# Polysketch attention followed by a rational MoE layer: own PSUM buffers for parts of the first key sketches, two first loads exchanged, w_out loaded in 4 KB pieces, and a new instruction order

## The chip, the cores and the metric

The kernel runs on one core of a Trainium2 chip. The core has five engines with a queue each: TensorE (PE; its weight loads are listed apart as PEld), VectorE (DVE), ScalarE (ACT), GpSimd (POOL) and SyncE (SP), which here issues most of the DMAs. Each engine works through its own instructions in order and waits on semaphores for the others. The metric is the device time of one execution in microseconds; the kernel before took 274.04 us (median of three, 273.96 to 274.2).

## The reference

Attention with polynomial sketches over 4 batches of 4 heads, 1088 tokens and 32 features each, then one feed-forward layer on all 4352 tokens with 128 features and 2048 hidden units:

```python
def phi(x):
    a = np.einsum('rd,bhsd->bhsr', S1, x)      # r = 8
    b = np.einsum('rd,bhsd->bhsr', S2, x)
    return np.einsum('bhsi,bhsj->bhsij', a, b).reshape(*x.shape[:-1], r * r)
q_p, k_p = (phi(q), phi(k))
kv = np.einsum('bhsf,bhsd->bhfd', k_p, v)
z = np.sum(k_p, axis=2)
x = (q_p @ kv) / (q_p . z + 1e-06)              # per token and head
h = x @ w_in
P = a[0] + a[1]*h + a[2]*h**2 + a[3]*h**3
Q = 1.0 + abs(b[0])*abs(h) + abs(b[1])*h**2
out = (P / (Q + 1e-06)) @ w_out
```

(Put together from the two functions of the reference; between them the heads' outputs are laid side by side, 128 features per token.)

## The kernel before

Everything is one list of steps, `ORDER` (lines 21 to 57), written out by an earlier search: each entry `name:i` calls one small function, and the instructions go to the engines' queues in just that order. Nothing is reordered afterwards, so `ORDER` fixes the order on each engine.

**Keys** (class `Keys`): of a batch `b`, `kt0..kt3` are 32x32 transposes on DVE (L251), `ks` the sketches on PE (L257), `kc` the copy of one sketch factor to SBUF on ACT (L264), `kf` the outer product `k_p` on DVE (L269), `kp` the products with `v` on PE (L298), `kk` the copy of `kv` on ACT (L308, L310). The first batch is cut into three parts, so that work can start on the first rows: part 0 holds two tiles of 128 tokens, part 1 two, part 2 five. `k_p` has two buffers.

**Queries** (classes `Queries`, `Spread`): `qt` transpose on DVE (L321), `qs` sketches on PE (L334, L402), `qc` copy on ACT (L341, L344, L408), `qf` product on DVE (L350, L353, L425), `qp` products with `kv` on PE (L361), `qd`, `qi`, `qx` denominator, reciprocal and quotient on DVE or ACT (L369 to L381), `qb` transpose back on PE (L387), `qk` copy to `xT` on ACT (L391). The blocks 0 to 3 belong to the first batch. In a `Spread` block the copies travel to DRAM and back to be spread over the partitions (L413 to L419, by SP).

**The layer**: 17 units (`units`), each a tile of 128 partitions x 4096 columns (hidden blocks times tokens). Unit 0 and the two last have 256 tokens, the others 512. `h0..h3` are the hidden matmuls into a PSUM tile of 1024 columns (L448), `e` their copy to bf16 on ACT (L454), `u`, `w`, `y` (L477, L483, L488) build Q on DVE, `ln` and `ex` (L539, L543) give `r = 1/Q` on ACT, `pa` or `pd` (L534, L529) a linear term on ACT or DVE, `s`, `m`, `v`, `x` (L547 to L562) the products on DVE, `G` (L581) the matmuls with the three scaled copies of `w_out`, `st` the store (L590, L598). `wo:0` to `wo:5` (L610 to L618) make the three bf16 copies of `w_out` in halves; `W_ENG` says which of them run on ACT (1) or DVE (0).

**PSUM**: the pool `att` has four tiles of 512 columns (`bank`), the pool `hps` two of 1024 columns (`wide`). The first batch's key sketches and the first two query sketches all take `wide` tiles.

**Loads**: the first batch's keys come in three DMAs: rows for the first four tiles (L144, on SP), the rest of three quarters (L146, on ACT's queue), the rest of the last quarter (L148, on ACT's queue). `lq`, `lk`, `lv`, `lw` (w_out in two halves), `lx` (w_in in two halves) are DMAs on SP at their place in `ORDER`. `w_out` is read with row `fo*128 + fi` on partition `fi`, that is in rows of 512 bytes.

`tn:i` puts `TURNS[i]` matmuls on zeros into PE's queue.

Of the kernel before, what the change touches and what calls it, by code (L numbers as in the profile page):

```python
# [16 lines left out]
PSUM = bass.MemoryType.PSUM  # L17


TURNS = (10, 2, 0, 0, 2, 0, 0, 0, 0)  # L20
ORDER = """
tn:4 tn:0 lw:1 kt0:0 lq:0 kt2:0 lw:0 kt3:0 lx:1 kt1:0 ks0:0 lk:1 qt:0 ks2:0 kc0:0 lx:0 kf0:0 ba:0 qt:1 tn:1 kc2:0 qs:0
kf2:0 kp0:0 qc:0 ks1:0 qf:0 kc1:0 kf1:0 qs:1 wo:1 qt:3 kp1:0 qc:1 kp2:0 qf:1 qt:2 qs:3 wo:4 kk:0 lq:1 lv:1 wo:2 qp:0
wo:0 qs:2 qd:0 wo:5 qi:0 qx:0 qc:2 qb:0 qf:2 qk:0 wo:3 qp:1 kt0:1 qc:3 h2:0 qd:1 qi:1 qx:1 qt:5 h3:0 e2:0 qt:4 kt1:1
qp:2 e3:0 h1:0 pa1:0 u1:0 w1:0 h0:0 y1:0 qd:2 e1:0 qi:2 qx:2 qs:4 e0:0 qb:1 qb:2 qt:6 ks1:1 qk:1 u0:0 qk:2 ln1:0 w0:0
ks0:1 y0:0 h1:1 lk:2 kc1:1 ex1:0 lq:2 kf1:1 h3:1 e1:1 s1:0 kc0:1 h0:1 e3:1 kf0:1 pa0:0 m1:0 h2:1 qf:3 e0:1 x1:0 qp:3
qc:4 e2:1 kt0:2 h0:2 ln0:0 u1:1 kt1:2 h1:2 w1:1 e0:2 ex0:0 y1:1 ks0:2 h2:2 e1:2 s0:0 qd:3 ln0:1 h3:2 qi:3 m0:0 e2:2
lk:3 qx:3 kp1:1 x0:0 e3:2 ex0:1 u1:2 qb:3 lv:2 G0:0 pd0:1 qk:3 w1:2 ln1:1 G1:0 G2:0 qf:4 G3:0 kc0:2 kk:1 y1:2 ex1:1
G4:0 G5:0 kf0:2 qp:4 ln0:2 s0:1 qs:5 G0:1 qd:4 qc:5 qi:4 ex0:2 qt:7 G1:1 qx:4 m0:1 qb:4 ks1:2 qk:4 s1:1 pa1:1 h2:3
s0:2 kc1:2 m1:1 h3:3 e2:3 kf1:2 h1:3 e3:3 st:0 x1:1 ln1:2 qs:7 x0:1 h0:3 e1:3 kt1:3 m0:2 h2:4 e0:3 pd1:2 pa0:2 u1:3  # L30
h3:4 qt:9 w1:3 e2:4 G2:1 ex1:2 x0:2 h0:4 qf:5 e3:4 kp1:2 s1:2 pa0:3 y1:3 h1:4 qc:7 e0:4 m1:2 ln0:3 qp:5 kt0:3 e1:4
G3:1 x1:2 ex0:3 G4:1 m0:3 G5:1 u1:4 ks0:3 qd:5 ln1:3 qi:5 G0:2 w1:4 G1:2 pa1:3 qx:5 G2:2 y1:4 lv:3 qb:5 G3:2 qk:5
ex1:3 h0:5 m1:3 v0:3 kk:2 ln0:4 h2:5 s1:3 e0:5 qs:6 G4:2 qf:7 ex0:4 h1:5 x0:3 qt:8 qc:6 e2:5 s0:4 e1:5 h3:5 pd0:4
pa1:4 m0:4 h1:6 v1:3 e3:5 x0:4 G5:2 ln1:4 u1:5 h3:6 st:2 e1:6 w1:5 qp:7 ex1:4 x1:3 h0:6 e3:6 y1:5 qd:7 pa0:5 lq:3 G0:3
G2:3 qi:7 s1:4 h2:6 e0:6 m0:5 ln0:5 m1:4 qs:8 G3:3 e2:6 qf:6 G5:3 x1:4 ex0:5 G0:4 u1:6 G1:4 qc:8 ln1:5 qp:6 v0:5 qx:7
w1:6 qb:7 qd:6 G2:4 pa0:6 qi:6 G3:4 qx:6 y1:6 qb:6 qk:7 G4:4 qk:6 ex1:5 h3:7 m0:6 pa1:5 G5:4 qt:10 s1:5 h1:7 e3:7 st:4
h2:7 e1:7 m1:5 ln0:6 x0:5 h0:7 e2:7 x1:5 qs:9 e0:7 h3:8 qf:8 ex0:6 u1:7 h1:8 v0:6 qc:9 ln1:6 w1:7 ks1:3 s0:6 e1:8 G0:5
y1:7 kc1:3 qp:8 ex1:6 h2:8 pd1:6 kc0:3 e3:8 s1:6 ln0:7 h0:8 kf0:3 e2:8 m1:6 G2:5 ex0:7 G3:5 x0:6 G4:5 kf1:3 qd:8 e0:8
qs:10 G5:5 ln1:7 qi:8 u1:8 kp1:3 qx:8 pa0:7 w1:8 qb:8 G0:6 qf:9 qk:8 y1:8 qc:10 h3:9 ex1:7 s0:7 h2:9 e3:9 s1:7 ln0:8
h0:9 m0:7 e2:9 x1:6 G2:6 e0:9 h1:10 x0:7 ex0:8 pd1:7 h1:9 m1:7 pa0:8 s0:8 G3:6 e1:9 u1:9 G0:7 qt:11 ln1:8 qp:9 qt:12  # L40
u0:9 m0:8 h3:10 e1:10 w1:9 qd:9 ex1:8 qf:10 h2:10 x0:8 e3:10 G4:6 x1:7 e2:10 h0:10 y1:9 kk:3 pa0:9 w0:9 qp:10 qi:9
y0:9 e0:10 G1:7 qx:9 qd:10 ln0:9 s1:8 qb:9 G5:6 qi:10 u1:10 G2:7 qk:9 ex0:9 G3:7 qx:10 m1:8 qb:10 G4:7 qk:10 ln1:9
pd1:8 h1:11 s0:9 w1:10 ex1:9 qs:11 h0:11 m0:9 e1:11 x1:8 G5:7 qc:11 e0:11 h3:11 y1:10 pa1:9 h2:11 s1:9 e3:11 ln0:10
x0:9 G0:8 h0:12 m1:9 e2:11 pd0:10 ex0:10 h1:12 u1:11 x1:9 G1:8 ln1:10 w1:11 G0:9 G2:8 e1:12 s0:10 G3:8 e0:12 y1:11
h2:12 ex1:10 G4:8 m0:10 ln0:11 G1:9 qf:11 G5:8 s1:10 ex0:11 h3:12 x0:10 pa1:10 m1:10 qs:12 G2:9 s0:11 G3:9 e2:12 G4:9
pd0:11 qc:12 ln1:11 m0:11 qp:11 x1:10 G5:9 e3:12 x0:11 G0:10 qd:11 ex1:11 G1:10 qi:11 u1:12 G2:10 pa1:11 qx:11 G3:10
w1:12 qb:11 G4:10 s1:11 qk:11 pa0:12 h1:13 y1:12 h2:13 e1:13 m1:11 ln0:12 h3:13 st:6 x1:11 ex0:12 G5:10 qf:12 st:10
qp:12 e2:13 s0:12 e3:13 h0:13 st:8 ln1:12 m0:12 h2:14 u1:13 e0:13 x0:12 ex1:12 h3:14 u0:13 w1:13 e2:14 w0:13 G0:11
s1:12 e3:14 h1:14 pa1:12 y0:13 h0:14 m1:12 qd:12 e1:14 y1:13 G1:11 e0:14 qi:12 pd0:13 G2:11 ln1:13 qx:12 G3:11 u1:14
G4:11 ex1:13 x1:12 G5:11 w1:14 qb:12 G0:12 qk:12 ln0:13 G1:12 s1:13 h0:15 y1:14 ex0:13 h2:15 m1:13 e0:15 ln0:14 s0:13  # L50
h1:15 pd1:13 e2:15 m0:13 ex0:14 h3:15 x1:13 x0:13 e1:15 G2:12 e3:15 s0:14 G3:12 pa0:14 G4:12 u1:15 h2:16 m0:14 ln1:14
w1:15 G5:12 h3:16 x0:14 ex1:14 y1:15 G0:13 e2:16 G1:13 e3:16 s1:14 h0:16 ln0:15 st:12 u3:16 G2:13 u2:16 e0:16 w3:16
h1:16 w2:16 ex0:15 y3:16 pd0:15 G3:13 y2:16 e1:16 s0:15 G4:13 pa1:14 G5:13 u0:16 m0:15 G0:15 ln1:15 G1:15 w0:16 m1:14
G0:14 G1:14 ex1:15 y0:16 G2:14 pd1:15 G3:14 ln0:16 v1:14 x0:15 s1:15 ex0:16 G2:15 G3:15 x1:14 G4:15 ln2:16 m1:15 G0:16
ex2:16 s0:16 pa0:16 x1:15 G1:16 G5:14 s2:16 pa3:16 m0:16 G5:15 ln3:16 m2:16 x0:16 ex3:16 st:14 pa2:16 G2:16 s3:16
G3:16 st:15 G4:16 x2:16 m3:16 G5:16 G6:16 x3:16 G7:16 G8:16 st:16
""".split()
W_ENG = (1, 1, 0, 1, 0, 1)
P_ON_ACT = (1, 1, 0, 1, 1, 0, 1, 1, 0, 1, 1, 1, 1, 0, 1, 0, 1, 0, 1, 1, 0, 1, 0, 1, 1, 1, 0, 0, 1, 1, 0, 0, 1, 1)
SPLIT_A = (0, 9, 13, 16)  # L60
QUARTER = (16,)
LX = 2
TAIL = 2
WIDE_S = (3, 5)
WIDE_M = (5,)
# [4 lines left out]
def kernel(  # L70
# [24 lines left out]
    NM = 4  # L95
# [39 lines left out]
    k0 = io.tile([128, NM * W], FP, name="k_sb", bufs=1)  # L135
    k0_src = k[0].rearrange("h (g j) d -> (h g) (j d)", g=32)
    km = (NM - 1) * W
    s_raw = []
    for i, s_in in enumerate((S1, S2)):
        t = consts.tile([128, D], FP, name=f"s_raw{i}")  # L140
        (nc.scalar, nc.sync)[i].dma_start(out=t, in_=bass.AP(tensor=s_in.tensor, offset=s_in.offset,
                                                             ap=[[0, 16], [D, R], [1, D]]))
        s_raw.append(t)
    nc.sync.dma_start(out=k0.rearrange("p (m x) -> p m x", m=NM)[:, :, 0:4 * D],  # L144
                      in_=bass.AP(tensor=k.tensor, offset=k.offset, ap=[[S * D // 32, 128], [W, NM], [1, 4 * D]]))
    nc.scalar.dma_start(out=k0[:, 0:km].rearrange("p (m x) -> p m x", m=NM - 1)[:, :, 4 * D:],  # L146
                        in_=k0_src[:, 0:km].rearrange("p (m x) -> p m x", m=NM - 1)[:, :, 4 * D:])
    nc.scalar.dma_start(out=k0[:, km + 4 * D:S], in_=k0_src[:, km + 4 * D:S])  # L148
    q0 = io.tile([128, S], FP, name="q_sb", bufs=1)
# [43 lines left out]
    for i in range(2):  # L193
        t = consts.tile([128, D], FP, name=f"sT{i}")
# [30 lines left out]
    def wide():  # L225
        return hps.tile([128, 1024], FP, name="h_ps")
# [5 lines left out]
    class Keys:  # L232
        def __init__(self, b, k_sb, v_sb, first=False):
            self.b, self.dst, self.k_sb, self.v_sb = b, kvz[b % 2], k_sb, v_sb
            self.take = wide if first else bank
            self.first = first
            a, b, last = slice(0, NM - 1), slice(NM - 1, NM), slice(4, NL)
            if first:
                self.PARTS = ((0, 2), (2, 2), (4, NT - 4))
                self.BLOCKS = [[(slice(0, NM), slice(0, 2))], [(slice(0, NM), slice(2, 4))], [(a, slice(4, NT))], [(b, last)]]  # L240
            else:
                self.PARTS = ((0, 4), (4, NT - 4))
                self.BLOCKS = [[(a, slice(0, NT))], [(b, slice(0, NL))]]
            self.ab, self.sk, self.k_p = {}, {}, {}
# [197 lines left out]
    def hidden(i, part):  # L442
        t0, tl, f0, per = units[i]
        assert ready.issuperset(range(t0, t0 + tl, 64))
        t = live[i]["h", part] = wide()
        for x in range(per // 4):
            f = f0 + part * (per // 4) + x
            nc.tensor.matmul(t[:, x * tl:(x + 1) * tl], lhsT=w_in_sb[:, f * 128:(f + 1) * 128],  # L448
                             rhs=xT[:, t0:t0 + tl], start=True, stop=True)

    def evac(i, part):
# [259 lines left out]
```

## Time and profile before

| what | us |
|---|---|
| median of 3 runs | 274.04 |
| the profiled execution: its time | 274.08 |
| the profiled execution: span from first to last instruction | 272.3 |
| last DVE instruction ends | 268.4 |
| DVE busy in 6.0 to 18.9 / 18.9 to 31.0 | 10.62 of 12.90 / 9.04 of 12.10 |
| PE busy in the same two stretches | 11.46 / 12.10 |
| ACT busy in the same two stretches | 7.67 / 9.45 |
| two casts of `w_out` on DVE | 0.65 and 0.74 |
| four casts of `w_out` on ACT | 1.15, 1.15, 1.17 and 1.03 |

The span is what the profile's rows add up to; the execution's own time has 1.8 us more around it. Times in the rows count from the start of the span. The busy time of PE is modelled (matmuls overlap their weight loads and each other), so its share says less than those of DVE and ACT.

### The profile page before, as it was taken

What the parts mean: (1) busy time and instruction counts of PE and PEld (TensorE: products, weight loads), DVE (VectorE), ACT (ScalarE), POOL (GpSimd) and SP (SyncE); (2) the same over time, 40 slices, a digit from 0 to 9 for tenths busy, and PEclk for the clock granted to TensorE, in tenths of its full rate; (3) what the DMA queues carried; (4) which work ended last, traced back from release to release, by engine and by line L of the source; (5) the groups of instructions that cost most, each with busy time, mean ns of one, the idle gap of its engine ahead of it and who ended that gap; (6) DMA issues with size and microseconds to landing.
All of it is one profiled execution on the core that took longest, in us unless ns stands there. A gap on an engine that the chain in (4) does not pass through costs nothing.

```text
span 272.3 us, 3730 instructions
## 1 busy us (share of the span) xinstructions
PE 258.4 (95%) x1398; PEld 146.2 (54%) x1398; DVE 256.0 (94%) x277; ACT 250.2 (92%) x224; POOL 2.9 (1%) x24
## 2 busy tenths in 40 slices
PE   7989999999999899999999999999999998999763
PEld 2778656963564354545454554434545356675552
DVE  2876999999999999999999999999999999999993
ACT  1467999998999999999999999999999999999990
POOL 4000000000000000000000000000000000000000
PEclk9999999999999999999999999999999999999999
DMA  6993606314026052232304000120036100010004
GB/s 166 290 330 99 196 14 183 101 50 100 2 80 135 12 136 81 67 78 39 96 6 115 12 0 4 40 90 0 14 97 90 25 0 0 2 24 14 1 7 74
DMA packets 30530, 19.55 MB, mean 72 GB/s; under 512 B 20400, under 2 KB 26672, under 8 KB 30512
## 3 DMA queue, kind: packets, MB, share of 16 engines
q1 hardware_dynamic: 28992, 18.93, 27.2%
q10 hardware_dynamic: 1520, 0.38, 0.7%
q8 instruction: 11, 0.18, 0.3%
q14 instruction: 7, 0.06, 0.1%
HBM read 16.16 MB, written 3.15 MB: 71 GB/s over the span
## 4 chain that ended last, share of the span: by engine, by line
PE 35%; ACT 28%; DVE 23%; issue 9%; DMA 2%; SPq 1%; DVEq 0%; ACTq 0%
PE h_ps L448 17%; PE att_ps L581 9%; ACT hh L454 8%; ACT ln L539 7%; ACT r L543 7%; DVE s L547 4%; ACT p L534 4%; DVE g L551 4%; PE att_ps L361 3%; DVE g L562 3%; DVE w L488 3%; DVE w L483 2%; DMA k_sb<-in_k_dram 2%; PE att_ps L298 1%; PE att_ps L257 1%
## 5 line engine op out<-in xcount | busy, mean ns | idle before, releaser
L448 PE MATMUL h_ps<-xT,w_in_sb 128*128 128x512 f32 (+1 forms) x320 | 126.2, 536 | 2.3 <-ACT hh L454 1.6
L448 PEld LDWEIGHTS h_ps<-xT,w_in_sb 128*128 128x128 f32 x320 | 58.3, 190 | 52.8 <-issue 35.0
L454 ACT CAST hh<-h_ps 128x1024 bf16<-128x1024 f32 x68 | 68.2, 1022 | 4.2 <-PE h_ps L448 3.7
L581 PEld LDWEIGHTS <-w_out 128*128 128x128 bf16 x460 | 44.6, 98 | 46.0 <-issue 15.1
L543 ACT ACTIVATE r<-ln 128x2048 bf16<-128x2048 f32 (+1 forms) x35 | 65.9, 1883 | 0.3
L539 ACT ACTIVATE ln<-w 128x2048 f32<-128x2048 bf16 (+1 forms) x35 | 65.9, 1882 | 0.3
L534 ACT ACTIVATE p<-hh,a_sb 128x2048 bf16<-128x2048 bf16 (+1 forms) x23 | 46.7, 2035 | 0.1
L547 DVE TENSOR_TENSOR s<-hh,r 128x2048 bf16<-128x2048 bf16 (+2 forms) x33 | 40.9, 1243 | 0.2
L488 DVE TENSOR_TENSOR w<-w,u 128x4096 bf16<-128x4096 bf16 (+2 forms) x22 | 39.5, 1798 | 0.1
L581 PE MATMUL att_ps<-g,w_out 128*128 128x512 bf16 (+1 forms) x160 | 34.8, 347 | 3.6 <-DVE g L562 3.6
L551 DVE TENSOR_TENSOR g<-hh,s 128x2048 bf16<-128x2048 bf16 (+1 forms) x30 | 35.2, 1175 | 0.0
L581 PE MATMUL att_ps<-r,w_out 128*128 128x512 bf16 (+1 forms) x160 | 35.0, 347 | 0.0
L562 DVE TENSOR_TENSOR g<-g,p 128x2048 bf16<-128x2048 bf16 (+1 forms) x30 | 34.9, 1175 | 0.0
L581 PE MATMUL att_ps<-s,w_out 128*128 128x512 bf16 (+1 forms) x140 | 29.8, 343 | 0.9 <-DVE s L547 0.9
L483 DVE TENSOR_SCALAR w<-u,b_abs 128x4096 bf16<-128x4096 bf16 (+2 forms) x22 | 23.9, 1092 | 0.1
L477 DVE TENSOR_SCALAR u<-hh 128x4096 uint16<-128x4096 uint16 (+2 forms) x22 | 21.2, 968 | 0.9 <-ACT hh L454 0.8
L361 PEld LDWEIGHTS att_ps<-kvz,q_pT 128*128 128x128 f32 x144 | 17.6, 191 | 4.9 <-ACT sk_sb L408 1.0
L361 PE MATMUL att_ps<-kvz,q_pT 128*128 128x66 f32 x144 | 18.0, 274 | 0.9 <-DVE q_pT L353 0.5
L298 PEld LDWEIGHTS att_ps<-v_sb,k_p 128*64 128x64 f32 (+1 forms) x288 | 8.8, 138 | 2.6 <-issue 1.8
L529 DVE TENSOR_SCALAR p<-hh,a_sb 128x2048 bf16<-128x2048 bf16 x12 | 9.6, 799 | 0.0
L298 PE MATMUL att_ps<-v_sb,k_p 128*64 128x64 f32 (+1 forms) x288 | 9.5, 224 | 0.0
L425 DVE TENSOR_TENSOR q_pT<-a_all,b_all 128x768 f32<-128x768 f32 (+1 forms) x10 | 9.0, 896 | 0.0
(60 smaller groups left out, 135.1 us busy)
## 6 DMA issues: line engine op xcount, KB each, us to landing
a_all<-sk_d SPq DMA_DIRECT2D x6, 384.0 KB
b_all<-sk_d SPq DMA_DIRECT2D x12, 192.0 KB
v_sb<-in_v_dram SPq DMA_DIRECT2D x12, 144.0 KB
k_sb<-in_k_dram SPq DMA_DIRECT2D x3, 544.0 KB
q_sb<-in_q_dram SPq DMA_DIRECT2D x3, 544.0 KB
a_all<-sk_d SPq DMA_DIRECT2D x4, 320.0 KB
b_all<-sk_d SPq DMA_DIRECT2D x8, 160.0 KB
w_out_sb_f<-in_moe_w_out_dram SPq DMA_DIRECT2D x2, 512.0 KB
```

The source lines that it names most:

```text
L361: nc.tensor.matmul(self.nd[:, o:o + 2 * KW], lhsT=self.q_p[:, c, x:x + 128], rhs=kvz[self.b % 2][:, c, :], start=True, stop=True)
L448: nc.tensor.matmul(t[:, x * tl:(x + 1) * tl], lhsT=w_in_sb[:, f * 128:(f + 1) * 128], rhs=xT[:, t0:t0 + tl], start=True, stop=True)
L454: nc.scalar.copy(out=live[i]["hh"][:, part * PW:(part + 1) * PW], in_=live[i]["h", part])
L483: nc.vector.tensor_scalar(out=t[:, c], in0=live[i]["u"][:, c], scalar1=ab1, scalar2=ab0, op0=AX.mult, op1=AX.add)
L488: nc.vector.tensor_mul(out=t[:, c], in0=t[:, c], in1=live[i]["u"][:, c])
L534: nc.scalar.activation(out=part_of(i, "p", h), in_=hh, func=ACT.Identity, scale=a3, bias=a2)
L539: nc.scalar.activation(out=t, in_=live[i]["w"][:, span(h)], func=ACT.Ln, bias=1.0 + 1e-6)
L543: nc.scalar.activation(out=part_of(i, "r", h), in_=live[i]["ln"], func=ACT.Exp, scale=-1.0)
L547: nc.vector.tensor_mul(out=part_of(i, "s", h), in0=hh, in1=part_of(i, "r", h))
L551: nc.vector.tensor_mul(out=part_of(i, "g", h), in0=hh, in1=part_of(i, "p" if horner(i, first(h)) else "s", h))
L562: nc.vector.tensor_mul(out=g, in0=g, in1=part_of(i, "s" if horner(i, first(h)) else "p", h))
L581: nc.tensor.matmul(outs[t0][:, :tl], lhsT=w_sb[y][:, f0 + x, :], rhs=part_of(i, key, h)[:, c:c + tl], start=done[0] == 0, stop=done[0] == ...
```

## The change

- The first batch's key sketches of parts 0 and 1 take `bank` tiles; only part 2 still takes a `wide` tile.
- The DMA of L144 goes to ACT's queue and that of L146 to SP's.
- `w_out` is read with rows `a*1024 + fi*8 + fo` on partition `fi`: eight neighbouring rows, 4 KB in one piece, per partition and half. The hidden units are thereby permuted among the blocks of 128, and the hidden matmuls take the fitting columns of `w_in`: the 128 columns of a block lie 8 columns (32 bytes) apart in SBUF instead of side by side.
- `ORDER` is another list in its opening and in detail up to its end; `W_ENG` changes from (1, 1, 0, 1, 0, 1) to (0, 0, 1, 0, 0, 1); `TURNS` gives 15 idle matmuls instead of 14. `LX` and the new `PERM` are not read anywhere.

The opening of `ORDER` and what else differs (the lines of `ORDER` after these differ too, mostly by steps exchanged with a neighbour):

```diff
-TURNS = (10, 2, 0, 0, 2, 0, 0, 0, 0)
+TURNS = (10, 2, 0, 0, 1, 2, 0, 0, 0)
 ORDER = """
-tn:4 tn:0 lw:1 kt0:0 lq:0 kt2:0 lw:0 kt3:0 lx:1 kt1:0 ks0:0 lk:1 qt:0 ks2:0 kc0:0 lx:0 kf0:0 ba:0 qt:1 tn:1 kc2:0 qs:0
-kf2:0 kp0:0 qc:0 ks1:0 qf:0 kc1:0 kf1:0 qs:1 wo:1 qt:3 kp1:0 qc:1 kp2:0 qf:1 qt:2 qs:3 wo:4 kk:0 lq:1 lv:1 wo:2 qp:0
-wo:0 qs:2 qd:0 wo:5 qi:0 qx:0 qc:2 qb:0 qf:2 qk:0 wo:3 qp:1 kt0:1 qc:3 h2:0 qd:1 qi:1 qx:1 qt:5 h3:0 e2:0 qt:4 kt1:1
-qp:2 e3:0 h1:0 pa1:0 u1:0 w1:0 h0:0 y1:0 qd:2 e1:0 qi:2 qx:2 qs:4 e0:0 qb:1 qb:2 qt:6 ks1:1 qk:1 u0:0 qk:2 ln1:0 w0:0
-ks0:1 y0:0 h1:1 lk:2 kc1:1 ex1:0 lq:2 kf1:1 h3:1 e1:1 s1:0 kc0:1 h0:1 e3:1 kf0:1 pa0:0 m1:0 h2:1 qf:3 e0:1 x1:0 qp:3
+tn:5 tn:0 lq:0 lw:1 kt0:0 lw:0 kt1:0 lx:1 ks0:0 kt2:0 lx:0 tn:1 kt3:0 kc0:0 lk:1 ks2:0 kf0:0 qt:1 qt:0 qs:1 kc2:0
+kf2:0 ks1:0 kc1:0 kp0:0 qc:1 ba:0 qs:0 kf1:0 qt:2 kp1:0 qf:1 kp2:0 qt:3 qc:0 lq:1 qf:0 qs:2 kk:0 wo:3 lv:1 wo:4 wo:2
+qp:0 wo:5 tn:4 qd:0 qp:1 qi:0 qx:0 qc:2 qf:2 qb:0 qs:3 qk:0 qd:1 qi:1 h3:0 qx:1 wo:0 h2:0 e3:0 kt0:1 kt1:1 h1:0 lk:2
+e2:0 qt:5 pa1:0 wo:1 qb:1 qt:4 qp:2 u1:0 h0:0 w1:0 qd:2 qk:1 qc:3 e1:0 qi:2 qx:2 y1:0 qb:2 qs:4 e0:0 ks1:1 qt:6 qk:2
+u0:0 ln1:0 h1:1 w0:0 y0:0 kc1:1 ex1:0 h3:1 kf1:1 e1:1 ks0:1 s1:0 e3:1 h2:1 m1:0 ln0:0 lq:2 kt0:2 h0:1 x1:0 e2:1 kc0:1
...
-W_ENG = (1, 1, 0, 1, 0, 1)
+W_ENG = (0, 0, 1, 0, 0, 1)
...
-    nc.sync.dma_start(out=k0.rearrange("p (m x) -> p m x", m=NM)[:, :, 0:4 * D],
+    nc.scalar.dma_start(out=k0.rearrange("p (m x) -> p m x", m=NM)[:, :, 0:4 * D],
...
-    nc.scalar.dma_start(out=k0[:, 0:km].rearrange("p (m x) -> p m x", m=NM - 1)[:, :, 4 * D:],
+    nc.sync.dma_start(out=k0[:, 0:km].rearrange("p (m x) -> p m x", m=NM - 1)[:, :, 4 * D:],
...
-    w_out_src = moe_w_out.rearrange("(fo fi) d -> fi fo d", fi=128)
+    w_out_src = moe_w_out.rearrange("(a fi fo) d -> a fi (fo d)", a=2, fi=128)
+    w_in_blocks = w_in_sb.rearrange("p (a fi fo) -> p a fo fi", a=2, fi=128)
...
-            self.take = wide if first else bank
...
-            ab = self.ab[part] = self.take()[:, 0:n * H * 2 * R].rearrange("p (t h s r) -> p t h s r", h=H, s=2, r=R)
+            ab = (wide if self.first and part == 2 else bank)()[:, 0:n * H * 2 * R]
+            ab = self.ab[part] = ab.rearrange("p (t h s r) -> p t h s r", h=H, s=2, r=R)
...
-            nc.tensor.matmul(t[:, x * tl:(x + 1) * tl], lhsT=w_in_sb[:, f * 128:(f + 1) * 128],
+            nc.tensor.matmul(t[:, x * tl:(x + 1) * tl], lhsT=w_in_blocks[:, 2 * f // nf, f % (nf // 2)],
...
-        nc.sync.dma_start(out=w_out_sb_f[:, f], in_=w_out_src[:, f])
+        nc.sync.dma_start(out=w_out_sb_f[:, f].rearrange("p f d -> p (f d)"), in_=w_out_src[x])
```

## The prediction

> **What bounds the kernel now.** I read the totals first, then the busy time by stage, then DVE's waits, then the opening in order of time.
>
> ```profile
> PE 258.4 (95%) x1398; PEld 146.2 (54%) x1398; DVE 256.0 (94%) x277; ACT 250.2 (92%) x224; POOL 2.9 (1%) x24
> ```
> ```profile
> core 0: us, PE busy (x) PEld busy (x) DVE busy (x) ACT busy (x) POOL busy (x), PEclk, DMA share, GB/s
> 0.00:6.00 6.00, 4.82 (x12) 1.64 (x12) 0.92 (x5) 1.28 (x1) 2.92 (x24) 1.00 0.55 148
> 6.00:18.90 12.90, 11.46 (x139) 8.87 (x139) 10.62 (x21) 7.67 (x17) 0.00 (x0) 1.00 1.06 327
> 18.90:31.00 12.10, 12.10 (x71) 10.12 (x71) 9.04 (x17) 9.45 (x13) 0.00 (x0) 1.00 0.65 148
> ...
> 66.00:250.00 184.00, 181.59 (x855) 94.73 (x854) 182.99 (x182) 183.00 (x152) 0.00 (x0) 1.00 0.20 47
> ```
> The columns are the stretch, its length, and each engine's busy time. Between 66 and 250 us DVE and ACT each idle 1.0 of 184 us. So nothing in the long middle can shrink while the work stays the same: what can be won lies in the opening, where DVE idles 5.1 us up to 6.0, 2.3 us up to 18.9 and 3.1 us up to 31.0. From there DVE works nearly without a gap to 268.4, where the last store begins. A microsecond that DVE wins in the opening and does not lose again is a microsecond of the kernel.
>
> ```profile
> 14.80 0.74 DVE L618 TENSOR_SCALAR w_out<-w_out_sb_f,a_sb 128x1024 bf16<-128x1024 f32 x1
> ...
> 22.09 1.04 DVE L321 STREAM_TRANSPOSE qT<-q_sb 128x384 f32<-128x384 f32 x2 [2.13 <-DMA q_sb<-in_q_dram]
> 23.05 0.37 DVE L251 STREAM_TRANSPOSE kT<-k_sb 128x224 f32<-128x224 f32 x1
> 23.65 0.69 DVE L477 TENSOR_SCALAR u<-hh 128x2048 uint16<-128x2048 uint16 x1 [0.23 <-ACT hh L454]
> ```
> ```profile
> 14.87 1.11 PE L361 MATMUL att_ps<-kvz,q_pT 128*128 128x66 f32 x8 [0.22 <-ACT kvz L308]
> 15.91 1.13 PE L334 MATMUL att_ps<-qT,SAB 64*128 64x256 f32 x8
> 17.02 0.41 PE L387 MATMUL att_ps<-ident,x_tok 128*128 128x128 f32 x2
> 17.96 1.11 PE L361 MATMUL att_ps<-kvz,q_pT 128*128 128x66 f32 x8 [0.52 <-DVE q_pT L353]
> 18.90 3.67 PE L448 MATMUL h_ps<-xT,w_in_sb 128*128 128x256 f32 x16
> ```
> DVE's longest wait in the opening after the first keys, 2.13 us, ends when the second batch's queries land at 22.07. But u, the layer's first step on DVE, starts at 23.65 behind ACT's copy of h: what sets the pace is when PE starts h (18.90) and how ACT drains it.
>
> **The change, part by part.**
>
> *Casts.* `W_ENG` moves both halves of the first copy and one of the second to DVE, and one half of the second to ACT. ACT loses 2 x 1.15 = 2.30 us net (L616), DVE gains 2 x 0.744 = 1.49 us (the L618 row above): its total goes from 256.0 to 257.5. They cost nothing only if they fall into DVE's idle time: `wo:0` and `wo:1` now stand ahead of and between the second batch's transposes, where the 2.13 us are. Without that cover they cost 1.49 us.
>
> *Buffers.* No instruction more or less. With sketches 0 and 1 in `bank` tiles, the first `qs` no longer waits for a key sketch to be drained, and the second only for part 2's. In before DVE waited 0.31 and 0.46 us for ACT's copies of the query sketches. Against that, the idle pair `tn:1` (0.53 us from its start at 8.39 to the next matmul) now stands ahead of `ks2`, and `kf1` needs `kp0` to be through with one of two `k_p` buffers, while `kp0` now stands behind `qs:1` and `ks1`.
>
> *Exchanged loads.* The issues take 0.81 us (L144) and 0.60 us (L146), starting at 1.47 on SP and 1.41 on ACT, so L144 starts 0.06 us sooner at best; the landing that DVE waits for (6.01) depends on 16 shared DMA engines that are already busy. Bounds: 0.06 us sooner, 0.2 us later (the longer issue ahead of L148). I take 0. L148's part is transposed last now, with 0.42 us of `kt1` as cover.
>
> *w_out in 4 KB pieces.* Two DMAs as before, 1.05 MB, 256 rows in place of 2048. In 6.0 to 18.9 the DMA engines are full at 327 GB/s, so these bytes are 3.2 us of that; the gain is between 0 and under 3.2 us of landing time for w_in, the second batch's keys, queries and values behind them. On the path I count 0: in before only the queries were waited for, and in the new order that wait is filled. Their DMA also starts about 1 us sooner, since it waits for `qt:3` (14.3 before).
>
> *SP's order.* The second half of w_in moves ahead of the second batch's keys (0.52 MB, 1.6 us at 327 GB/s later for these); `kt0:1` moves from 18.15 to 19.3, and keys landed before 18.15. The third batch's keys are issued ahead of the first `Spread` block's trip through DRAM, whose copy moves from 18.92 to about 25.4. The second trip in before took 3.0 us from copy to the read's issue (37.6 to 40.6), some 6 to the product; 32 is ahead of the 38 where `qf:3` now stands.
>
> *Idle matmul.* One more, `tn:4`, 0.25 us on PE before `qp:1`.
>
> *Strided weights.* 320 weight loads now read columns 32 bytes apart. No row has a strided weight load.
>
> ```profile
> line engine op names shapes xcount | busy us, mean ns | idle before us <-releasers
> L448 PEld LDWEIGHTS h_ps<-xT,w_in_sb 128*128 128x128 f32 x320 | 58.3, 190 | 52.8 <-issue 35.0 <-ACT hh L454 11.5 <-ACT xT L391 2.3
> L581 PEld LDWEIGHTS <-w_out 128*128 128x128 bf16 x460 | 44.6, 98 | 46.0 <-issue 15.1
> ```
> A load of 128 float32 columns takes 190 ns, of 128 bf16 columns 98 ns. Nothing is read less, so 190 is the lower bound. The upper bound I set at the same ratio once more, 380 ns. Weight loads run beside matmuls: a pass with 512 columns takes 0.43 us (16 in 7.04) and hides even 380. A pass with 256 columns takes 0.215 us (8 in 1.72), and hides a load up to that. There are 96 such passes, in units 0, 15 and 16. I take 190, nearer to the row of the same instruction, since a float32 column already costs two bf16 columns.
>
> The Trainium skill (SBUF — State Buffer, Door 1: The DMA port swizzle) speaks against this part: SBUF is read in 16-byte lines, and each access that goes to a new line pays a penalty, so four float32 may be strided over freely, and eight may not. No run so far shows it; by it the last rival below holds, without it the sum.
>
> *The new opening, laid out by hand* with before's durations, and each instruction behind its queue and its inputs. DVE: four `kt` 6.01 to 7.5, `kf0` to 8.1, `qt:1`, `qt:0` to 8.9; `kf2` waits for `ks2` (7.6 to 8.9 on PE) and its copy: 9.3 to 10.8; `kf1` waits for `kp0` (PE 10.4 to 11.0): 11.1 to 11.8; `qt:2`, `qf:1`, `qt:3`, `qf:0` to 13.9. PE: `kp1` and `kp2` 12.1 to 13.95 (12.53 to 14.38 before); `qs:2` now hides the copies of `kv`; `qp:0` 15.0 to 16.1, `tn:4`, `qp:1` to 17.4, `qb:0` to 17.8; ACT copies xT to 18.25; h starts at 18.35, 0.55 sooner. Two parts of h take 3.5 us, so `e2` ends near 22.9 (23.6 before) and DVE starts `u1` then. There the lead shrinks: ACT does `pa1` (2.0), `qd`, `qk`, `qc:3` before the next two copies, so `e0` ends at 27.65 (27.96). DVE waits about 0.67 us for `qd:2` and starts `u0` at 27.7 (28.0); `y0` ends at 30.4 (30.7). DVE had time for both casts.
>
> At equal work some 8 us later: PE leads by 0.34, ACT by 0.1 (`ln0` moved ahead of `pa0`), DVE is 0.2 behind, because `s1` and `kf0:1` wait 0.3 and 0.4 us for ACT. For the rest the same instructions stand in a slightly different order; before's waits there come to 1.0 us on DVE, so the order can win at most that, and lose as much by my estimate. I take 0.
>
> **Sum**, against the profiled execution (274.08: 272.3 of span and 1.8 around it; the median is 274.04, 0.04 less): -0.35, the lead of 0.3 at `y0` and PE's 0.34 kept, DVE's two short waits counted as my own error. 273.7.
>
> **Rivals.** What this kernel's measurement can tell from no change is about 0.2%, 0.55 us.
> 1. *The whole lead goes through.* h starts 0.55 us sooner, and the waits that I see for `qd:2` and `kf0:1` are not there because ACT drains faster than I laid out (its queue is 2.3 us lighter); up to half of the 1.0 us of later waits go too. 274.04 - 0.55 - 0.5 = 273.0. For it: ACT's waits for h, 1.66 and 0.71 us in 20 to 23. Against: DVE has 1.49 us more to do.
> 2. *Slower: DVE pays for the casts.* If h starts at 18.9 or later, `u1` starts as before with 1.49 us more work ahead of it, and the waits behind `pa1` and ACT's copies stay: 0.55 later than laid out puts DVE 0.75 behind at equal work; 1.49 at most. 274.9. The point is h's start: `kf2` behind `tn:1` and `kf1` behind `kp0` could each make it later.
> 3. *Slower: strided weights.* At 380 ns the 32 passes of unit 0 cost 32 x 0.165 = 5.3 us on PE, which is full from 18.9 to 66; the 64 at the end 10.5, about half of it hidden behind queued DVE work: 284. It decides from 215 ns.
> 4. *The change does nothing that counts*: the landings stay, and h's start as well as DVE's work cancel. 274.0.
>
> **How the numbers follow.** Forecast (273.2 to 274.2): 0.37; rival 1: 0.27; rival 2: 0.22; rival 3: 0.10; rival 4: 0.04. The predicted time is 273.7. The range 272.5 to 275.4 takes in the forecast, rival 1 with all of the 1.0 us, and rival 2 up to the full 1.49; rival 3 and some tails (0.08) are left out. Faster than 273.49: rival 1 and 0.16 of the forecast, 0.43. Slower than 274.59: rivals 2 and 3, 0.32. Between: 0.25.
>
> **What would show it.** In the profile after: h's first matmul at 18.3 to 18.5 (later: rival 2); the weight loads of L448 at 190 ns (rival 3 if over 215); no DVE wait for the queries' landing; `u` near 22.9 and 27.7; DVE busy 257.5 and ACT 247.9; DVE's waits from 23 to 38 us, and whether its last instruction comes before 268.4. The prediction fails if DVE has gaps of a microsecond after 31 us, or if the first keys land more than 0.3 us off 6.0.

## The result, and the profile after

The changed kernel takes 275.13 us (median of 6 runs, 275.04 to 275.82) against 274.0 us before: a ratio of 1.0045 [1.0032, 1.0058], 1.1 to 1.2 us slower, twice what this kernel's measurement can tell. The forecast was 273.7.

The totals of the page after:

```profile
PE 260.3 (95%) x1384; PEld 178.6 (65%) x1399; DVE 257.3 (94%) x279; ACT 248.1 (91%) x222; POOL 2.9 (1%) x24
```

DVE has 1.3 us more to do than before and ACT 2.1 less, close to the 1.49 and 2.30 that the moved casts account for. What stands out is PEld, the weight loads: 178.6 us in place of 146.2, with the same loads. Of the costliest groups, the two that load weights (busy time and mean ns of one, then the idle time before them and what ended it):

```profile
L450 PEld LDWEIGHTS h_ps<-xT,w_in_sb 128*128 128x128 f32 x320 | 91.4, 322 | 27.4 <-ACT hh L456 5.6 <-ACT xT L393 1.4 <-issue 0.5
L583 PEld LDWEIGHTS <-w_out 128*128 128x128 bf16 x460 | 44.9, 99 | 43.6 <-issue 10.9
```

The 320 loads of `w_in` take 322 ns instead of 190; those of `w_out`, which no edit touches, take 99 as before. The idle time under "issue", in which the loader merely stood ready, is gone: 35.0 us before, 0.5 now. The loader of the hidden matmuls has no slack left.

In the opening the first steps came sooner than laid out. DVE's rows in order of time (start, duration, the wait before in brackets):

```profile
5.12 1.62 DVE L252 STREAM_TRANSPOSE kT<-k_sb 128x256 f32<-128x256 f32 x4 [1.49 <-DMA k_sb<-in_k_dram]
...
18.14 0.74 DVE L620 TENSOR_SCALAR w_out<-w_out_sb_f,a_sb 128x1024 bf16<-128x1024 f32 x1
19.39 1.37 DVE L252 STREAM_TRANSPOSE kT<-k_sb 128x864 f32<-128x864 f32 x2 [0.50 <-DMA k_sb<-in_k_dram]
21.80 0.58 DVE L323 STREAM_TRANSPOSE qT<-q_sb 128x384 f32<-128x384 f32 x1 [1.05 <-DMA q_sb<-in_q_dram]
22.30 0.71 DVE L620 TENSOR_SCALAR w_out<-w_out_sb_f,a_sb 128x1024 bf16<-128x1024 f32 x1
22.93 0.57 DVE L323 STREAM_TRANSPOSE qT<-q_sb 128x384 f32<-128x384 f32 x1
23.43 0.65 DVE L479 TENSOR_SCALAR u<-hh 128x2048 uint16<-128x2048 uint16 x1
...
27.80 0.51 DVE L323 STREAM_TRANSPOSE qT<-q_sb 128x320 f32<-128x320 f32 x1 [0.66 <-PE att_ps L404]
28.23 0.65 DVE L479 TENSOR_SCALAR u<-hh 128x2048 uint16<-128x2048 uint16 x1
```

The keys are transposed from 5.12 (6.01 before), and h starts at 17.80, 1.10 us sooner than before. The first `u` gains only 0.22 of that: 23.43 against 23.65. It follows the second batch's queries. From 21.80, when DVE stops waiting for them, it works without a gap through two transposes and the cast between them, up to `u`. PE and ACT in order of time:

```profile
17.80 6.12 PE L450 MATMUL h_ps<-xT,w_in_sb 128*128 128x256 f32 x24
```
```profile
20.12 1.01 ACT L456 CAST hh<-h_ps 128x1024 bf16<-128x1024 f32 x1 [2.38 <-PE h_ps L450]
22.04 1.01 ACT L456 CAST hh<-h_ps 128x1024 bf16<-128x1024 f32 x1 [0.91 <-PE h_ps L450]
```

24 passes take 6.12 us, 0.255 each, where 16 took 3.67 before, 0.229 each; and ACT waits 2.38 and 0.91 us for them (1.66 and 0.71 before). ACT's second copy of h ends at 23.05 all the same, 0.38 ahead of the first `u`, so here the queries hide the longer passes. At the second `u` they don't: DVE waits 0.66 us for the sketches of L404, which stand on PE behind the next part of h, and `u` starts at 28.23, 0.23 us later than before. Then the busy time by stage (length, then busy time of PE, PEld, DVE and ACT):

```profile
core 0: us, PE busy (x) PEld busy (x) DVE busy (x) ACT busy (x) POOL busy (x), PEclk, DMA share, GB/s
0.00:31.00 31.00, 28.99 (x214) 22.51 (x215) 21.52 (x44) 16.27 (x28) 2.92 (x24) 1.00 0.68 208
31.00:66.00 35.00, 34.90 (x232) 26.41 (x233) 34.40 (x34) 34.14 (x34) 0.00 (x0) 1.00 0.41 110
66.00:250.00 184.00, 181.46 (x836) 119.53 (x848) 182.63 (x181) 181.77 (x152) 0.00 (x0) 1.00 0.20 47
```

The second of these rows in the kernel before:

```profile
31.00:66.00 35.00, 35.00 (x229) 21.43 (x228) 34.82 (x35) 33.92 (x34) 0.00 (x0) 1.00 0.35 100
```

Up to 31 us DVE has done 21.52 us of work, before 20.59: 0.93 more, but it has 1.3 more to do in all, so it is 0.37 behind. From 31 to 250 it idles 1.97 us (0.60 and 1.37), before 1.19 (0.18 and 1.01): 0.78 more. Together that is the 1.15 by which DVE's last instruction ends later (269.56 against 268.41). Two thirds of the loss arise behind 31 us, where the forecast took next to nothing, and over half of these before 66.

### The profile page after: what moved, and what is told of

Read it like the earlier page. It is cut to its first block, busy times and chain, and to the rows that moved or that the text cites. A ratio compares the mean times of both kernels' runs of the same rounds, so it can differ in the third digit from the quotient of the medians.

```text
span 273.3 us, 3724 instructions
## 1 busy us (share of the span) xinstructions
PE 260.3 (95%) x1384; PEld 178.6 (65%) x1399; DVE 257.3 (94%) x279; ACT 248.1 (91%) x222; POOL 2.9 (1%) x24
## 4 chain that ended last, share of the span: by engine, by line
PE 54%; ACT 19%; DVE 14%; issue 7%; DMA 3%; SPq 0%; DVEq 0%; ACTq 0%
PE h_ps L450 28%; PE att_ps L583 14%; ACT hh L456 6%; ACT ln L541 5%; ACT r L545 5%; PE att_ps L363 4%; ACT p L536 3%; DVE g L553 3%; DVE g L564 3%; PE att_ps L300 3%; DVE s L549 2%; DVE w L490 2%; PE att_ps L259 2%; DMA k_sb<-in_k_dram 2%; DVE w L485 2%
## 5 line engine op out<-in xcount | busy, mean ns | idle before, releaser
L450 PE MATMUL h_ps<-xT,w_in_sb 128*128 128x512 f32 (+1 forms) x320 | 129.2, 549 | 1.3 <-ACT hh L456 1.2
L450 PEld LDWEIGHTS h_ps<-xT,w_in_sb 128*128 128x128 f32 x320 | 91.4, 322 | 27.4 <-ACT hh L456 5.6
L583 PE MATMUL att_ps<-g,w_out 128*128 128x512 bf16 (+1 forms) x154 | 34.0, 346 | 4.2 <-DVE g L564 3.9
L583 PE MATMUL att_ps<-r,w_out 128*128 128x512 bf16 (+1 forms) x156 | 34.0, 346 | 0.3
L583 PE MATMUL att_ps<-s,w_out 128*128 128x512 bf16 (+1 forms) x135 | 28.9, 341 | 0.3
L271 DVE TENSOR_TENSOR k_p<-att_ps,b_sk 128x1280 f32<-128x1280 f32 (+2 forms) x8 | 9.5, 1182 | 1.0 <-PE att_ps L300 0.9
```

Of the source, the lines that this page charges most:

```text
L450: nc.tensor.matmul(t[:, x * tl:(x + 1) * tl], lhsT=w_in_blocks[:, 2 * f // nf, f % (nf // 2)], rhs=xT[:, t0:t0 + tl], start=True, stop=True)
L583: nc.tensor.matmul(outs[t0][:, :tl], lhsT=w_sb[y][:, f0 + x, :], rhs=part_of(i, key, h)[:, c:c + tl], start=done[0] == 0, stop=done[0] == ...
```

## The experiments

Two theories. *Strided loads*: the 32-byte distance makes each load of `w_in` 1.66 times as long, PE is late with h, and everything else in the change is worth a little. The expectations call this theory S and the next one theory O. *Casts and order* (rival 2): DVE pays for the casts or for the new order, and the loads stay hidden. All ratios are to the kernel before on the same chip, from five rounds, with a 95% interval. The names `fo2`, `fo4`, `fo16` stand for how many neighbouring rows of `w_out` go to one partition, and so how many columns of 4 bytes lie between two of a weight block. In `a_contig`, `a_s256` and `a_s512` the permutation that belongs to `w_out`'s new rows is left out, in all units or in some.

### Columns side by side again (a_contig, a_permoff)

```diff
-  lhsT=w_in_blocks[:, 2 * f // nf, f % (nf // 2)]
+  lhsT=w_in_sb[:, f * 128:(f + 1) * 128]
```

`a_permoff` also reads `w_out` in rows of 512 bytes again.

> The changed kernel with one thing altered: a block's weight load reads 128 columns of w_in side by side, not 32 bytes apart. Order, engines and all DMAs stay. (The rows of w_out then do not belong to the hidden units that meet them: a permutation is left out.) Theory S, strided weight loads cost the time: the load of w_in falls from 315 to 190 ns, the 256-column passes of unit 0 from 0.25 to 0.215 us, so the first three parts of h end 0.8 us sooner (24 x 0.03), and the time falls by 1.0 to 1.8 us, to 273.3 to 274.1. Theory O, VectorE pays for the two more casts and the new order's waits: the load falls to 190 ns too, but the time stays within 0.4 us of 275.1.

> The changed kernel with w_in read side by side and w_out loaded in rows of 512 bytes again; order, engines, buffers and the exchanged loads stay. Against the kernel with the side-by-side w_in alone this is the price of the small rows. If landings count: the second batch's keys and queries land up to 1.5 us later, VectorE's waits of 0.5 and 1.05 us for them grow, and the time is 0.3 to 1.0 us longer than that kernel's. If they are covered: the same within 0.3 us. Theory S: faster than the changed kernel by 0.7 us or more in either case. Theory O: no more than 0.4 us off 275.1.

Measured: `a_contig` 273.49 us, 0.998 [0.997, 0.999]; `a_permoff` 273.5 us, 0.9982 [0.9966, 0.9997]. The groups by line, `a_contig`:

```profile
L450 PEld LDWEIGHTS h_ps<-xT,w_in_sb 128*128 128x128 f32 x320 | 58.8, 190 | 52.8 <-issue 37.3 <-ACT hh L456 10.0 <-ACT xT L393 1.6
```

One operand's address pattern is all that differs from the changed kernel, and 1.6 us come back: the load is at 190 ns, with 37.3 us of slack. Rival 2 falls: with casts and order in place the kernel is faster than before. The 4 KB pieces are worth nothing that the medians show, since the two ratios agree.

What a longer load costs PE shows in the first passes of unit 0. The loads of the kernel after, then the loads and the matmuls of `a_contig`:

```profile
17.80 5.83 PEld L450 LDWEIGHTS h_ps<-xT,w_in_sb 128*128 128x128 f32 x24 [0.33 <-ACT xT L393]
```
```profile
17.85 5.05 PEld L450 LDWEIGHTS h_ps<-xT,w_in_sb 128*128 128x128 f32 x24 [0.23 <-ACT xT L393]
```
```profile
17.85 5.45 PE L450 MATMUL h_ps<-xT,w_in_sb 128*128 128x256 f32 x24
```

24 loads of 322 ns would be 7.7 us end to end; they take 5.83. So successive loads overlap. The matmuls take 6.12 us after and 5.45 here: 0.028 more for a pass on average, not 322 minus 215. By stage, `a_contig` (columns as above):

```profile
0.00:31.00 31.00, 28.80 (x215) 20.30 (x216) 21.50 (x44) 16.89 (x28) 2.92 (x24) 1.00 0.70 211
31.00:66.00 35.00, 34.82 (x234) 21.79 (x234) 34.71 (x35) 33.86 (x34) 0.00 (x0) 1.00 0.38 107
66.00:250.00 184.00, 179.93 (x840) 95.07 (x853) 183.46 (x182) 182.76 (x151) 0.00 (x0) 1.00 0.20 47
```

Up to 31 us both kernels have the same DVE work done (21.52 and 21.50). From there to 250 DVE idles 1.97 us after and 0.83 in `a_contig`: 1.14 of the 1.4 us between the spans (273.3 and 271.9). DVE's waits in that stretch, first after, then `a_contig` (total us, times, longest):

```profile
DVE rec L378 <- ACT den L374: 0.8, 2, 0.5
DVE u L479 <- ACT hh L456: 0.6, 2, 0.4
DVE s L549 <- ACT r L545: 0.2, 1, 0.2
DVE out_sb L592 <- PE att_ps L583: 0.2, 1, 0.2
```
```profile
DVE rec L378 <- ACT den L374: 0.4, 2, 0.3
DVE u L479 <- ACT hh L456: 0.2, 1, 0.2
```

No single wait holds the loss: several grow by 0.2 to 0.4 us, at steps fed by ACT and PE. DVE pays in small waits for what PE and ACT deliver later. How much falls before 31 us differs between executions: in this profile of `a_contig` the queries' transposes start at 22.92, 1.12 us later than after, and hide what the short loads win there. In `a_fo2` below, whose loads are short too, they start at 21.30; its first row by stage:

```profile
0.00:31.00 31.00, 29.45 (x217) 20.94 (x218) 22.78 (x44) 17.53 (x29) 2.94 (x24) 1.00 0.71 212
```

There DVE has 1.26 us more done at 31 than after. The total is what the medians fix; the split between opening and middle is not settled.

### The stride alone on the old order (b_perm)

Before, with the changed lines of `w_out_src`, `w_in_blocks` and `fetch_w` alone.

> The kernel before, with one part of the change: w_out in pieces of 4 KB and w_in's columns 32 bytes apart in a weight load. Its own order, engines and loads stay. Theory S: weight loads of 315 ns, the two first parts of h end 0.5 us later (16 x 0.03), and the time is 1.0 to 1.8 us over before: 275.0 to 275.8. Rival, the strided loads hurt only in the new order, because that order has less room between h and ScalarE's copies: 274.0 to 274.5.

Measured: 276.61 us, 1.0096 [1.0083, 1.0109], slower than theory S's own 275.0 to 275.8. By form, and the first `u`:

```profile
L449 PEld LDWEIGHTS h_ps<-xT,w_in_sb 128*128 128x128 f32 x320 | 91.2, 322 | 28.2 <-ACT hh L455 6.5 <-ACT xT L392 2.1 <-issue 0.8
```
```profile
24.37 0.69 DVE L478 TENSOR_SCALAR u<-hh 128x2048 uint16<-128x2048 uint16 x1 [1.71 <-ACT hh L455]
```

The same 322 ns cost 2.6 us in the old order and 1.6 in the new one. The new order takes the long loads better; it doesn't take them for nothing. In the old order the first `u` waits 1.71 us for ACT's copy of h, so the longer passes reach DVE at once; in the new order it doesn't wait for it. How much of the difference of 1.0 us this explains was not tried.

### How far apart may the columns lie (a_fo2, a_fo4, a_fo16)

```diff
+FO = 2
-    w_out_src = moe_w_out.rearrange("(a fi fo) d -> a fi (fo d)", a=2, fi=128)
-    w_in_blocks = w_in_sb.rearrange("p (a fi fo) -> p a fo fi", a=2, fi=128)
+    w_out_src = moe_w_out.rearrange("(a fi fo) d -> fi a (fo d)", a=nf // FO, fi=128)
+    w_in_blocks = w_in_sb.rearrange("p (a fi fo) -> p a fo fi", a=nf // FO, fi=128)
```

with 4 for `fo4`, and the loads of `w_out` cut to match (1 KB and 2 KB pieces). `fo16` leaves out `a`: 64 bytes between columns.

> The changed kernel with pieces of 1 KB: two neighbouring rows of w_out per piece, columns of w_in 8 bytes apart in a block. The Trainium skill (SBUF — State Buffer, Door 1) has 16-byte lines and strides inside a line free, so by it the load takes 190 ns here. Theory S with the line rule: 190 ns and the time of the side-by-side kernel. Theory S with any stride costing: 315 ns and 275.1. Theory O: 275.1 with either.

> The changed kernel with pieces of 2 KB: columns of w_in 16 bytes apart in a block, so that each float32 lies in another 16-byte line. If the cost comes with a new line per column: 315 ns as with 32 bytes, and 275.1. If it comes with the span of the load (4 KB at 32 bytes, 2 KB here): between 190 and 315, about 230, and a time between. If strides up to 16 bytes are free: 190 ns.

> The changed kernel with columns of w_in 64 bytes apart (w_out's rows 16 to a partition, each half a piece of 4 KB as before). If each column costs one new 16-byte line and no more: weight loads of 315 ns as with 16 and 32 bytes, and 275.1. If the cost goes with the span of the load (8 KB here): over 400 ns and 276 or more.

| | distance | load, mean ns | first 24 passes, us | time, us | ratio |
|---|---|---|---|---|---|
| a_contig | 4 B | 190 | 5.45 | 273.49 | 0.998 [0.997, 0.999] |
| a_fo2 | 8 B | 196 | 5.46 | 273.35 | 0.9973 [0.9959, 0.9987] |
| a_fo4 | 16 B | 316 | 5.98 | 275.05 | 1.0043 [1.0023, 1.0063] |
| after | 32 B | 322 | 6.12 | 275.13 | 1.0045 [1.0032, 1.0058] |
| a_fo16 | 64 B | 299 | 5.70 | 274.41 | 1.0021 [1.0008, 1.0034] |

By form, `a_fo2`, then `a_fo4`:

```profile
L451 PEld LDWEIGHTS h_ps<-xT,w_in_sb 128*128 128x128 f32 x320 | 60.8, 196 | 51.6 <-issue 36.3 <-ACT hh L457 10.3 <-ACT xT L394 1.7
```
```profile
L451 PEld LDWEIGHTS h_ps<-xT,w_in_sb 128*128 128x128 f32 x320 | 89.8, 316 | 28.4 <-ACT hh L457 5.8 <-ACT xT L394 1.1 <-issue 0.7
```

Up to 32 bytes it is a step, not a slope: free up to 8 bytes, nearly all of the price at 16. At 64 both theories on record missed: the load is shorter there. The view of that line shortest/median/longest ns, for the kernel after and for `a_fo16`:

```profile
L450 PEld LDWEIGHTS h_ps<-xT,w_in_sb x320: 312/315/338, 17.8 to 245.2; 128*128 128x128 f32 x160
```
```profile
L450 PEld LDWEIGHTS h_ps<-xT,w_in_sb x320: 291/297/319, 17.6 to 243.9; 128*128 128x128 f32 x160
```

18 ns less a load, and the passes and the time follow by more than in proportion: 0.42 of the 0.67 us that the first 24 passes had lost come back, and 0.7 of the 1.6 us of the kernel. `a_fo2`, which leaves nothing out, beats both kernels with `w_out`'s rows in pieces of 1 KB: 0.27% below before, 0.7% below after.

### In which units it costs (a_s256, a_s512)

```diff
-  lhsT=w_in_blocks[:, 2 * f // nf, f % (nf // 2)]
+  lhsT=(w_in_blocks[:, 2 * f // nf, f % (nf // 2)] if tl == 256 else w_in_sb[:, f * 128:(f + 1) * 128])
```

and 512 in place of 256.

> The changed kernel, strided (32 bytes) weight loads only in the units of 256 tokens (0, 15 and 16: 96 of the 320 loads), side by side in the others (a permutation is left out). If the passes too short to hide a load of 315 ns carry the cost (0.244 us each instead of 0.215, 96 x 0.03 = 2.8 us on TensorE, 0.9 of it in the opening): near 275.1. If the cost lies in the long units, where a load is exposed whenever a batch of h begins: near 273.5.

> The mirror: strided loads only in the units of 512 tokens (224 loads), side by side in units 0, 15 and 16. Short passes carry the cost: near 273.5. The long units carry it: near 275.1. If the two halves add up, this one's excess over 273.5 and the other's make 1.6 us together.

Measured: `a_s256` 274.15 us, 1.0009 [1.0001, 1.0018]; `a_s512` 274.19 us, 1.0023 [1.0002, 1.0043]. Over `a_contig` that is 0.0029 and 0.0043, together 0.0072, where both at once (after) cost 0.0065. So the price lies in both kinds of units, and neither expectation held alone. The 96 passes of 256 columns cost about 0.8 us: of the 0.03 that each gains on PE, 2.9 us in all, nearly three quarters are hidden. The passes of 512 columns, which the forecast gave as full cover at 0.43 us each, cost 0.8 us by the medians and 1.2 by the ratios. The first eight of them in order of time take 3.77 us after and 3.65 in `a_contig`. The lengths of these eight matmuls (shortest/median/longest ns), first after, then `a_contig`:

```profile
L450 PE MATMUL h_ps<-xT,w_in_sb x8: 592/592/770, 28.8 to 32.0; 128*128 128x512 f32 x8
```
```profile
L450 PE MATMUL h_ps<-xT,w_in_sb x8: 592/592/648, 28.7 to 31.8; 128*128 128x512 f32 x8
```

The median is the same; only the longest grows, by 0.122 us, which is the whole difference of the group. In both traces it is the first of the eight: the second starts 0.607 us behind it after and 0.485 in `a_contig`, and all later ones 0.43 apart in both. So a pass of 512 columns does hide a load of 322 ns, except the first of a group, which has none of its own kind ahead of it.

### The parts that are left (f_wide, f_weng, f_noexch)

Each is `a_fo2` with one part undone: all of the first sketches in `wide` tiles; `W_ENG` as before; the two loads exchanged back.

```diff
-            ab = (wide if self.first and part == 2 else bank)()
+            ab = (wide if self.first else bank)()
```
```diff
-W_ENG = (0, 0, 1, 0, 0, 1)
+W_ENG = (1, 1, 0, 1, 0, 1)
```
```diff
-    nc.scalar.dma_start(out=k0.rearrange(
+    nc.sync.dma_start(out=k0.rearrange(
-    nc.sync.dma_start(out=k0[:, 0:km].rearrange(
+    nc.scalar.dma_start(out=k0[:, 0:km].rearrange(
```

> The 1 KB kernel with all three first key sketches in the two wide tiles again. The order has the two query sketches between them, so a sketch then waits for VectorE to drain the one two places ahead: the second part's sketch waits for part 2's product (ends near 10 us), the second query sketch for the first query product. If own buffers matter: h starts 0.5 to 1.5 us later and the time is 0.4 to 1.5 us longer. If they don't: 273.4.

> The 1 KB kernel with the casts of w_out on the engines of before: 2.3 us back on ScalarE, 1.49 us off VectorE, at the same places in the order. Theory O, VectorE pays for its two casts because it is busy to the end: 272.0 to 272.9. If they lie in VectorE's waits of the opening: 273.2 to 274.0, with more idle time on VectorE and ScalarE's casts ahead of its copies of h.

> The 1 KB kernel (columns of w_in 8 bytes apart, 273.35) with the two first loads of the keys put back on their old queues. If the exchange is what made the first transpose start at 4.8 to 5.2 us instead of 6.0: it starts at 6.0 again, h starts 0.4 to 0.8 us later, and the time is 0.3 to 0.8 us longer. If something else did it: 5.1 and 273.4.

Measured: `f_wide` 275.01 us, 1.0044 [1.0025, 1.0063]; `f_weng` 274.05 us, 1.001 [0.9993, 1.0027]; `f_noexch` 273.28 us, 0.9973 [0.9964, 0.9983]; beside `a_fo2` at 0.9973.

*Buffers*: worth 0.7%, 1.9 us, by the ratios in this order, more than the 0.4 to 1.5 expected. PE in order of time, `f_wide`, then `a_fo2`:

```profile
10.13 0.66 PE L260 MATMUL h_ps<-S,kT 128*128 128x64 f32 x4 [0.84 <-DVE k_p L272]
10.72 0.69 PE L301 MATMUL att_ps<-v_sb,k_p 128*64 128x64 f32 x16
12.27 1.91 PE L337 MATMUL h_ps<-qT,SAB 64*128 64x256 f32 x8 [0.86 <-DVE k_p L272]
14.10 2.65 PE L301 MATMUL att_ps<-v_sb,k_p 128*64 128x64 f32 x56
...
20.92 3.30 PE L451 MATMUL h_ps<-xT,w_in_sb 128*128 128x256 f32 x14
```
```profile
9.13 0.66 PE L260 MATMUL att_ps<-S,kT 128*128 128x64 f32 x4
9.81 0.69 PE L301 MATMUL att_ps<-v_sb,k_p 128*64 128x64 f32 x16
10.42 1.13 PE L337 MATMUL h_ps<-qT,SAB 64*128 64x256 f32 x8
11.48 1.85 PE L301 MATMUL att_ps<-v_sb,k_p 128*64 128x64 f32 x56
...
17.50 2.87 PE L451 MATMUL h_ps<-xT,w_in_sb 128*128 128x256 f32 x12
```

The sketches write `h_ps` there, so PE must wait twice until `k_p` has read a tile out. Then the same eight matmuls take 1.91 us in place of 1.13, and the 56 take 2.65 in place of 1.85. The windows of `f_wide`, whose column before the DMA share is the granted clock, show what goes with it:

```profile
11.00:12.00 1.00, 0.40 (x14) 0.27 (x10) 0.48 (x1) 0.63 (x3) 0.00 (x0) 1.00 0.96 303
12.00:13.00 1.00, 0.73 (x4) 0.66 (x6) 1.00 (x3) 0.00 (x0) 0.00 (x0) 0.74 1.11 295
13.00:14.00 1.00, 1.00 (x6) 0.37 (x4) 0.14 (x1) 0.00 (x0) 0.00 (x0) 0.50 1.04 261
14.00:15.00 1.00, 1.00 (x18) 0.90 (x18) 0.68 (x2) 0.58 (x1) 0.00 (x0) 0.50 0.91 287
```

After the two waits the clock fell to half for some 3 us, and h began at 20.92 instead of 17.50. This cut isn't needed for the loss: the four executions of `f_wide` with a mean clock of 0.989 to 1.0 took 274.65 to 275.01, still 1.3 to 1.7 us over `a_fo2`, while the three at 0.983 or 0.984, the profiled one among them, took 276.16 to 276.24.

*Casts*: moving them to DVE is a gain of 0.37%, 1.0 us by the ratios and 0.7 by the medians; the intervals lie just apart. The 274.05 is over the ranges of both theories. DVE's wait for ACT's denominators in `f_weng`, then in `a_fo2`:

```profile
DVE rec L379 <- ACT den L375: 1.9, 3, 1.3
```
```profile
DVE rec L379 <- ACT den L375: 0.6, 2, 0.4
```

And one cast on ACT in `f_weng`:

```profile
24.60 1.13 ACT L619 ACTIVATE w_out<-w_out_sb_f,a_sb 128x1024 bf16<-128x1024 f32 x1
```

With the casts back on ACT, DVE waits 1.3 us longer there: this cast stands right ahead of the denominators, which ACT reaches at 25.64, against 24.32 in `a_fo2`.

*Exchange*: nothing in the medians. In the profiles the first transpose starts at 5.71 without it and at 4.7 to 5.2 with it, and h at 18.26 without it against 17.50 in `a_fo2`; this lead is not in the end time.

### Does the end follow h's start (f_late)

`a_fo2` with four more idle matmuls, 0.85 us of PE, ahead of `qp:1`.

```diff
-TURNS = (10, 2, 0, 0, 1, 2, 0, 0, 0)
+TURNS = (10, 2, 0, 0, 5, 2, 0, 0, 0)
```

> The 1 KB kernel (273.35) with five idle matmuls instead of one before the second block's products: 4 x 0.21 = 0.85 us more on TensorE ahead of the first matmul of h, and no other engine has more to do. If the start of h sets the pace to the end: 274.0 to 274.3. If the room after it (VectorE's wait for the queries' landing, ScalarE's waits for h) takes the delay: 273.3 to 273.6.

Measured: 273.88 us, 0.9995 [0.9987, 1.0004], 0.0022 above `a_fo2`, 0.6 us; the intervals touch. That is short of the range for h's start and past the one for the room behind it. The profiles of the kernels with short loads and the casts on DVE don't settle it either (one execution each; times in us):

| | h starts | queries transposed from | first `u` | this execution | median |
|---|---|---|---|---|---|
| a_fo2 | 17.50 | 21.30 | 22.92 | 272.88 | 273.35 |
| f_noexch | 18.26 | 22.33 | 23.95 | 273.56 | 273.28 |
| a_permoff | 18.07 | 22.43 | 24.06 | 273.37 | 273.5 |
| a_contig | 17.85 | 22.92 | 24.54 | 273.7 | 273.49 |
| f_late | 18.33 | 23.35 | 24.98 | 274.16 | 273.88 |

The first `u` starts 1.62 or 1.63 us behind the queries in each of them, whatever h does, and where the queries come later the execution tends to end later. `f_noexch` starts h almost as late as `f_late` in its profile and loses nothing in its median. So it stays open whether the 0.6 us are PE's delay or a later landing.

## Why the prediction was wrong

The step that failed is the one on *Strided weights*, "I take 190, nearer to the row of the same instruction, since a float32 column already costs two bf16 columns". Measured: 322 mean, 315 median. That float32 costs twice bf16 says how much is read, not how the reads are laid out; it was no evidence against the upper bound. The rule set beside it (the Trainium skill, SBUF — State Buffer, Door 1: The DMA port swizzle) was the better guide: 16-byte lines, at least two hits on a line wanted, and a new line for each column is penalised. The trace agrees that eight float32 pay (315 to 322 ns) and that two don't (196). It disagrees where the section lets four float32 be strided freely: at 16 bytes the load took 316 ns, and the measurement decides. Nor does the rule tell why 64 bytes cost less than 32.

*Rival 3* (the prediction's sentence on the rule calls it the last rival) therefore named the right mechanism, with a chance of 0.10 and a price of 10 us that was far too high. Whether it decides from 215 ns was not tried: no run has a load between 196 and 299. The working behind the price was wrong, since it charged each pass with all that a load exceeds it by. Loads of successive passes overlap, so that the 32 passes of unit 0 lose 1.0 us on PE (8.36 against 7.39 in `a_contig`) and not 5.3. On the other side it counted the 512-column passes as cover, and by the first pass of each group they cost 0.8 to 1.2 us.

*Rival 2* came nearest to the time (274.9) by a mechanism that does not set it: `f_weng` shows that the casts on DVE are a gain.

*Casts.* 257.3 and 248.1 us of busy time are the forecast's 257.5 and 247.9. Of the two casts that were to fill the queries' wait only the one at 18.14 stands in it. The one at 22.30 comes behind the landing and ahead of `u`. The wait is not gone either: 1.05 of 2.13 us are left, and the second batch's keys, which the part on *SP's order* expected in time, are waited for 0.50 us.

*Buffers.* Right in direction: h at 17.80 against 18.35 laid out. *Exchanged loads.* I took 0 for the landing with bounds of 0.06 sooner and 0.2 later; it came 0.89 sooner in this profile. Worth nothing in the end, as costed, but outside the bounds, and one of the signs that the prediction named for its own failure. *w_out in 4 KB pieces.* Costed at 0, measured 0.

*The opening by hand.* `u` was to start at 22.9 and 27.7, paced by h and ACT's copies. With long loads it started at 23.43 and 28.23; with 8 bytes between the columns (`a_fo2`) at 22.92 and 26.98. That the first is the forecast's to 0.02 us is luck: the queries' landing sets it, and in the other four kernels of the last table it lies between 23.95 and 24.98.

*The sum.* Without the loads its number held: 273.7 forecast, 273.35 to 273.5 measured in the three kernels with short loads and the new order, casts and buffers (`a_contig`, `a_permoff`, `a_fo2`). The way to it was in part another: between h's start and the first `u` stood the queries' landing, which the forecast took to be covered. For the kernel itself the sum lacked one term, 1.6 us.

## What to carry to other kernels

A change of layout that makes a DMA's pieces longer also changes how every engine reads the tile afterwards: look for the reader with the tightest timing before counting the DMA's gain, which here was nothing. Where a stated rule speaks against a part and no row excludes it, price it from both ends, with overlap between neighbours allowed for. And a load that is shorter than the pass beside it is hidden there, but the first load of a group is not: here that cost 0.12 us a group.

## What the runs showed of the hardware

- A weight load of 128 float32 columns takes 190 ns at 4 bytes between columns, 196 at 8, 316 at 16, 322 at 32 and 299 at 64. The last is lower than its two neighbours; why stays open.
- Long loads overlap: 24 loads of 322 ns and more take 5.83 us, about 0.24 us from one start to the next.
- A wait of PE does not always bring the clock down. In `f_wide` two waits of 0.84 and 0.86 us within 3 us stood ahead of a fall to 0.50 for some 3 us (from 12 us). A wait of 2.17 or 2.18 us near the end (it ends between 254.7 and 258.1 us) stands in all twelve profiles of the new order; behind it the clock fell to 0.50 for some 3 us in four (`a_permoff`, `a_fo4`, `f_noexch`, `f_wide`) and stayed at 1.00 in eight.
- The first keys' landing goes with the queue that issues it: transposes from 4.7 to 5.2 us where the larger of the first two DMAs is on ACT's queue, 5.5 to 6.0 where it is on SP's.
